# Another order for a recorded list of 6007 calls, and output stores that SyncE issues nearly alone

## The chip, the cores and the metric

The kernel runs on one core of a Trainium2 chip. A core has a matrix engine (TensorE, PE in the profile), three engines that work on 128 partitions of on-chip memory (VectorE or DVE, ScalarE or ACT, GpSimd or POOL), and a sync engine (SyncE or SP) that only issues DMA transfers and waits. Each runs its own list of instructions in order; they meet at semaphores. ScalarE and GpSimd can issue DMAs too. TensorE writes into PSUM (eight banks, used here as four rooms of two banks), and VectorE or ScalarE must copy the result to SBUF before the room can be used again; such a copy is called an evacuation below. The metric is the device time of one execution in microseconds (us), the median of several runs.

## The reference

Two long convolutions over L = 2048 positions for 448 channels are mixed by a gate, with x = `A_u` (2048 by 448, bfloat16):

```python
g = _sigmoid((x * gate_w).sum(-1, keepdims=True))
a = _A_ref(x, A_A_re, A_A_im, A_B_re, A_B_im, A_C_re, A_C_im, A_log_dt, A_Dskip)
b = _B_ref(x, B_k, B_v, B_shift_k, B_ssm_k, B_ssm_D)
return g * a + (1 - g) * b
# _A_ref: P = exp(dt*A*l); K = einsum("dn,dnl,dn->dl", C, P, dt*B).real   (256 modes, l < 2048)
#         y = irfft(rfft(u padded) * rfft(K padded))[:2048] + u * Dskip
# _B_ref: kv = (4-tap convolution of k with shift_k) * v
#         y = irfft(rfft(kv padded) * rfft(ssm_k padded))[:2048] + kv * ssm_D;  b = q * y, with q = x
```

So convolution A first has to make its own filter K from 256 complex modes per channel, and convolution B takes its filter as an input.

## The kernel before

**Transforms by matmuls.** A sequence of 2048 positions is held as 32 by 64, and the Fourier transforms are two stages of small matmuls with constant matrices: `spread` (matrix Wc), `transform` (W2), a product of two spectra on VectorE, then `stage_a` (R) and `stage_b` (G) back. `swapped` exchanges the two halves of the partitions by eight SyncE DMAs of 112 KB (`q<-q` in the profile). Nearly every matmul group ends with an evacuation PSUM to SBUF, and nearly all SBUF buffers lie in one tile of eight slots, named `q` in the profile.

**Quarters and plan.** The 448 channels are worked on in four quarters H = 0 to 3. A list, PLAN, gives the order in which the steps are recorded: T0, B0, B1, T1, B2, A0, T2, B3, p2, A1, T3, A2, m0, p3, A3. T is `table(H)`, which makes the filter of A: `exps` and `levels` on ScalarE (Exp, then Sin, with `minus` negating a part of the tile `ET`), `tables` as some 60 multiplies and adds on VectorE over the tiles TQ and TP, then matmuls (`sums`, `gather`, `spread_in`). B and A are the two convolutions of a quarter, p and m products with the gate. Before the plan stand the constants, the parameters (`Modes.run` transposes the six raw parameters and multiplies them into `hold`), and the short convolution of k, whose taps are loaded from `B_shift_k`, and whose transposed k lies where u (`natu`) is loaded afterwards.

**The gate.** 112 matmuls add up x * gate_w (calls 715 to 826, `ps<-natu,q`), one evacuation copies the sums to `gx` (call 827), one matmul adds partitions, and ScalarE takes a tanh into `gt` (call 829).

**The last stage.** `stage_b_shared` makes the quarters A1 to A3 together in six chunks of rows, b0 = 0, 12, 24, 36, 48 (12 rows each) and 60 (four rows). The function `together` evacuates each chunk to `natu` (128x1008, or 128x336 for the last four rows), multiplies it by the gate and adds it to `natv` on VectorE, and `store` writes it out in four DMAs, one for each 32 partitions (84 KB, or 28 KB).

**What sets the order.** Building the kernel first records all calls, numbered 0 to 6006, in a list. `Order.issue` then issues them in the sequence of the string ORDER, and chains each instruction to the one before it on its engine, so that the string alone decides each engine's order. This is why every row of the profile names line 153, the issuing line. Three more strings hold one character for each decision: SLOTS the slot of each SBUF buffer, ROOMS the PSUM room, and SIDES whether an evacuation (or a step of `levels`) goes to VectorE (V) or ScalarE (S). ScalarE must load a table before it can change between Exp or Tanh and Sin (`ACT_TABLE_LOAD`); copies need none. These loads are not in the string: they stand wherever the order changes from one kind to the other.

Of the kernel before, what the change touches and what calls it, by code (L numbers as in the profile page):

```python
# [40 lines left out]
    "3414351063757536613442666006711745305010456674026664531672"  # L41
)
ROOMS = (
    "23103002012223210321303300123103121213010301202302011203300011220312010002301113132311322332103320231330111003123323"
    "023300130213120112220103120310033231332213101032220302021200231110332111213100313200213312002"
)
SIDES = (
    "SSSSSSSSSSSSSSSSSSSSSSSSSSSSSSSSSSSSSSSSSSSSSVSSSSSSSSSSSSSSSSSSVVSVVVSSSSSSSSSSSSSSSSSSSSSSSSSSSSSSSSSSSSSSSSSSSSSS"
    "VVVVVVSSSSSSSSSSSSSSSSSSSSSSSSSSSSSSSSSSSSSSSSSVSSSSSSVVVVVVSSSSVSSVSSSSSSSSSSSSSSSSSSSSSSSSSSSVSSSSSSVSSSSSSS"
)  # L50
ORDER = (
# [688 lines left out]
def body(  # L740
# [20 lines left out]
    nc = Order(tc)  # L761
# [144 lines left out]
    ug = vt  # L906
# [33 lines left out]
    def store(b0, n):  # L940
        for g in range(4):
            dmae[g % 2].dma_start(out4[g][:, b0:b0 + n, :], ug[g * 32:(g + 1) * 32, b0:b0 + n, :])
# [132 lines left out]
```

## Time and profile before

| what | value |
|---|---|
| median of 3 runs (lowest to highest) | 245.65 us (245.57 to 247.34) |
| profiled execution | 246.74 us, its span 245.0 us |
| VectorE busy | 221.1 us, 370 instructions |
| ScalarE busy | 216.5 us, 301 instructions |
| TensorE busy | 199.1 us, 5134 matmuls |
| GpSimd busy | 23.7 us, 83 instructions |
| TensorE clock granted, mean | 0.962 |
| read from and written to device memory | 8.17 MB and 2.52 MB |

The span runs from the first to the last recorded instruction of the profiled execution; what lies around it is not in the trace. "Busy" adds up the time in which an engine was executing. Rows of the timeline give the start, the length, the engine, the operation with output and inputs and the shape, and in brackets how long the engine had been idle before, with what ended the wait. Rows of groups give the count, the busy time, the mean of one in ns, and the idle time before them.

### The profile page before, as it was taken

How to read it: one execution, taken by the hardware profiler on the slowest of the kernel's cores; microseconds unless marked ns; L12 is line 12 of the kernel's file. 1: busy time of each engine (PE TensorE's matmuls, PEld its weight loads, DVE VectorE, ACT ScalarE, POOL GpSimd, SP SyncE). 2: the span in 40 equal slices, each digit the busy share in tenths (PEclk: the TensorE clock that was granted, in tenths of full speed). 3: DMA queues.
4: the chain of work that ended last, by engine and by line, in shares of the span. 5: the costliest groups of instructions: out<-in, count | busy, mean ns of one | idle time of the engine just before them, and what ended most of it. 6: DMA issues, size and time to landing. Idle time of an engine off the chain costs nothing.

```text
span 245.0 us, 11464 instructions
## 1 busy us (share of the span) xinstructions
PE 199.1 (81%) x5134; PEld 177.4 (72%) x5134; DVE 221.1 (90%) x370; ACT 216.5 (88%) x301; POOL 23.7 (10%) x83
## 2 busy tenths in 40 slices
PE   0786888794989898986789989986999899889940
PEld 0732688784879798976688879985999888789730
DVE  7999998999679999999999999996999999878570
ACT  3899999899599999999999999989999979859550
POOL 8700001020000010200000111000012220000000
PEclk9997999799799999999999999997999999999995
DMA  6999999999430548445033756300073357130177
GB/s 141 200 188 198 159 134 162 168 169 234 131 99 5 136 82 145 80 95 138 5 49 62 168 108 137 90 5 4 5 152 80 78 96 172 42 80 3 21 155 126
DMA packets 59040, 26.37 MB, mean 108 GB/s; under 512 B 49648, under 2 KB 57328, under 8 KB 58992
## 3 DMA queue, kind: packets, MB, share of 16 engines
q1 hardware_dynamic: 52256, 18.65, 41.0%
q0 software_dynamic: 2160, 5.51, 12.8%
q10 hardware_dynamic: 4576, 1.49, 3.2%
q8 instruction: 40, 0.66, 1.2%
q14 instruction: 8, 0.07, 0.1%
HBM read 8.17 MB, written 2.52 MB: 44 GB/s over the span
## 4 chain that ended last, share of the span: by engine, by line
ACT 43%; DVE 22%; PE 16%; DMA 8%; issue 5%; SPq 3%; POOL 1%; ACTq 1%; DVEq 0%; POOLq 0%
ACT q L153 32%; PE ps L153 16%; DVE q L153 7%; DVE TP L153 6%; ACT ET L153 5%; DMA q<-q 4%; DMA q<-in_B_ssm_k_dram 4%; SPq L153 3%; ACT L153 2%; DVE natv L153 2%; DVE TQ L153 2%; DVE G L153 2%; DVE ET L153 2%; ACT natu L153 1%; ACT natv L153 1%
## 5 line engine op out<-in xcount | busy, mean ns | idle before, releaser
L153 ACT CAST q<-ps 128x1024 bf16<-128x1024 f32 (+4 forms) x182 | 149.2, 941 | 10.9 <-PE ps L153 9.7
L153 PEld LDWEIGHTS <-q 128*64 128x64 bf16 (+3 forms) x1168 | 65.4, 133 | 22.6 <-issue 10.0
L153 DVE TENSOR_TENSOR TQ<-TQ,ET 128x896 bf16<-128x896 bf16 (+2 forms) x70 | 45.8, 685 | 0.0
L153 PE MATMUL ps<-q,s_W 128*128 128x112 bf16 (+1 forms) x544 | 35.0, 214 | 6.7 <-ACT q L153 4.7
L153 DVE TENSOR_TENSOR q<-q 128x896 bf16<-128x896 bf16 (+2 forms) x32 | 37.6, 1202 | 1.4 <-ACT q L153 1.4
L153 PE MATMUL ps<-TP,TQ 128*32 128x32 bf16 x1792 | 33.2, 241 | 3.3 <-issue 1.7
L153 PEld LDWEIGHTS <-s_W 128*128 128x128 bf16 x544 | 28.5, 99 | 9.9 <-issue 7.3
L153 PE MATMUL ps<-sa_R,q 128*128 128x128 bf16 x448 | 32.4, 228 | 2.3 <-ACT q L153 0.7
L153 PEld LDWEIGHTS <-TQ 128*32 128x32 bf16 x1792 | 30.1, 153 | 5.6 <-issue 3.2
L153 DVE TENSOR_TENSOR TP<-TP,ET 128x1792 bf16<-128x1792 bf16 (+3 forms) x25 | 31.6, 1272 | 0.0
L153 PEld LDWEIGHTS <-natu 128*32 128x32 bf16 (+1 forms) x560 | 28.8, 183 | 3.7 <-issue 3.2
L153 POOL DMA_DIRECT2D TP<-TP x15 | 13.0, 867 | 151.8 <-PE ps L153 72.0
L153 ACT ACTIVATE q<-hold 128x224 bf16<-128x224 f32 x64 | 23.3, 438 | 0.7 <-DVE hold L153 0.7
L153 PEld LDWEIGHTS <-G 128*128 128x128 bf16 x512 | 16.4, 96 | 3.0 <-DVE q L153 0.7
L153 PE MATMUL ps<-q,G 128*128 128x56 bf16 (+2 forms) x512 | 17.4, 187 | 0.7 <-ACT q L153 0.7
L153 ACT ACTIVATE ET<-q 128x1344 bf16<-128x1344 int16 (+1 forms) x12 | 17.5, 1468 | 0.1
L153 DVE TENSOR_TENSOR TP<-TP,q 128x3584 bf16<-128x3584 bf16 (+1 forms) x10 | 16.4, 1645 | 0.0
L153 PE MATMUL ps<-Wc,natu 128*64 128x128 bf16 x224 | 15.8, 283 | 0.3 <-ACT q L153 0.2
L153 PE MATMUL ps<-Wc,natv 128*64 128x128 bf16 x224 | 15.0, 290 | 1.0 <-ACT q L153 1.0
L153 PEld LDWEIGHTS <-natv 128*64 128x64 bf16 x224 | 14.3, 213 | 1.6 <-DVE natv L153 0.5
L153 PE MATMUL ps<-q,natu 128*32 128x224 bf16 (+3 forms) x336 | 14.2, 283 | 1.5 <-ACT q L153 1.0
L153 DVE TENSOR_TENSOR TQ<-TQ 128x448 bf16<-128x448 bf16 (+2 forms) x35 | 15.2, 445 | 0.0
(75 smaller groups left out, 221.2 us busy)
## 6 DMA issues: line engine op xcount, KB each, us to landing
q<-q SPq DMA_DIRECT2D x64, 112.0 KB, 2.7
TP<-TP POOLq DMA_DIRECT2D x9, 448.0 KB, 5.5
natv<-in_B_v_dram SPq DMA_DIRECT2D x4, 448.0 KB, 7.4
q<-in_B_ssm_k_dram SPq DMA_DIRECT2D x16, 112.0 KB, 4.5
natu<-in_A_u_dram SPq DMA_DIRECT2D x4, 448.0 KB, 9.9
TP<-TP POOLq DMA_DIRECT2D x6, 224.0 KB, 3.5
out_dram<-natv SPq DMA_DIRECT2D x10, 84.0 KB, 2.8
out_dram<-natv ACTq DMA_DIRECT2D x10, 84.0 KB, 3.1
```

The lines of the kernel that those rows point to most:

```text
L153: ins = f(*args, **{k: x.ap() if isinstance(x, Both) else x for k, x in kw.items()})
```

## The change

SLOTS, ROOMS, SIDES and ORDER are replaced, and one line of `store` is changed. The list of recorded calls, their shapes and the plan are the same.

```diff
@@ store (and the strings SLOTS, ROOMS, SIDES, ORDER, not shown)
     def store(b0, n):
         for g in range(4):
-            dmae[g % 2].dma_start(out4[g][:, b0:b0 + n, :], ug[g * 32:(g + 1) * 32, b0:b0 + n, :])
+            (dmae[g % 2] if b0 in (0, 48) else nc.sync).dma_start(out4[g][:, b0:b0 + n, :], ug[g * 32:(g + 1) * 32, b0:b0 + n, :])
```

Of 24 stores SyncE issued 12 and ScalarE 12; now SyncE issues 20 and ScalarE four (two of chunk 0, two of chunk 48).

By SIDES, eleven operations move from ScalarE to VectorE: the copy of the gate sums (128x64), two negations of `ET` in T0 (128x896 and 128x672), two spreads of B0 and B1 (128x512), one 128x896 copy of A1's transform, four copies of the last 40 us (128x896, 128x1024 and two of 128x448), and the evacuation of the chunk b0 = 24. Three move the other way: a negation of `ET` in T1 (128x896), a 128x896 copy of A1 and a 128x448 copy of T3.

By ORDER, every engine's sequence changes throughout. Three places follow, with the issuing line printed as L153 before and L152 after.

The first is the start of the program on ScalarE. `TP<-TP 128x64` and `sa_R<-TP` are sines for constants, `TP<-TQ` an exponential of log_dt, `q<-hold` the exponentials of T0 and T1, `ET<-q` their sines, `s_W` and `TQ<-ps` sines for the matrices W2 and G, `q<-ps 128x896` evacuations. Before:

```order
2 L153 ACT_TABLE_LOAD
3 L153 ACTIVATE TP<-TP 128x64 x2
4 L153 ACT_TABLE_LOAD
5 L153 ACTIVATE TP<-TQ 128x448
6 L153 DMA q<-in_B_shift_k_dram 128x1792
7 L153 ACTIVATE q<-hold 128x224 x11
8 L153 COPY TQ<-ps_77 128x1792
9 L153 ACTIVATE q<-hold 128x224 x2
10 L153 ACTIVATE q<-q,quarter 128x3x224
11 L153 ACTIVATE q<-hold 128x224 x4
12 L153 ACT_TABLE_LOAD
```

The next table load of before stands at row 32, behind all of these sines. After, first the beginning and then the part with the loads between the sines:

```order
2 L152 ACT_TABLE_LOAD
3 L152 ACTIVATE TP<-TQ 128x448
4 L152 ACTIVATE q<-hold 128x224 x13
5 L152 COPY TQ<-ps_77 128x1792
6 L152 DMA q<-in_B_shift_k_dram 128x1792
7 L152 ACTIVATE q<-hold 128x224 x3
8 L152 ACTIVATE q<-q,quarter 128x4x224
9 L152 ACT_TABLE_LOAD
10 L152 ACTIVATE ET<-q 128x4x448
```

```order
19 L152 ACTIVATE ET<-q 128x3x448
20 L152 ACT_TABLE_LOAD
21 L152 ACTIVATE q<-hold 128x224 x2
22 L152 ACTIVATE q<-q,quarter 128x3x224
23 L152 ACT_TABLE_LOAD
24 L152 ACTIVATE ET<-q 128x3x448
25 L152 ACTIVATE TP<-TP 128x64
26 L152 ACT_TABLE_LOAD
27 L152 ACTIVATE q<-hold 128x224
28 L152 CAST q<-ps_79 128x896
29 L152 ACTIVATE q<-hold 128x224
30 L152 ACT_TABLE_LOAD
```

Up to the first evacuations the program has four table loads before and seven after (one more at row 36), and in all 9 before and 12 after. The load of the taps has moved behind the copy of the parameters (`TQ<-ps_77`): its buffer shares a slot with the raw A and B parameters now. On SyncE the loads of u stand, as before, behind the loads of B's filters.

The second place is the gate. Before, ScalarE copies the sums to `gx` (`q<-hold` exponentials, `q<-ps` evacuations; the tanh is `gt<-ps_77`):

```order
68 L153 ACTIVATE q<-hold 128x224 x3
69 L153 CAST q<-ps_76 128x128x4
70 L153 COPY gx<-ps_77 128x64
71 L153 CAST q<-ps_79 128x128x8
72 L153 ACTIVATE gt<-ps_77 128x64
73 L153 ACT_TABLE_LOAD
```

After, the copy is among VectorE's rows (TQ and TP rows are T0's tables, `q<-hold` the first level of T1):

```order
101 L152 TENSOR_TENSOR TP<-TP,q 128x3584
102 L152 TENSOR_TENSOR TQ<-TQ 128x448
103 L152 TENSOR_TENSOR TQ<-TQ,ET 128x2x2x224
104 L152 COPY gx<-ps_79 128x64
105 L152 TENSOR_TENSOR TQ<-TQ,ET 128x2x2x224
106 L152 CAST q<-ps_76 128x128x4
107 L152 TENSOR_SCALAR q<-hold 128x224 x3
```

VectorE copies the gate sums itself, near the end of T0's tables, and the evacuation of 128x512 that stood before the copy on ScalarE has come with it. On TensorE the gate sums stood in two pieces, 715 to 778 and 779 to 826, with the calls 1658 to 1665 and 1934 to 1941 (transforms of B0 and B1) between them and 1743 to 1758 (a spread of B1) behind. Now these 32 matmuls stand ahead, and all 112 gate sums stand in one piece behind them.

The third place is the end of the program on ScalarE and VectorE, the chunks of the last stage: `natu<-ps` is an evacuation, `natu<-natu,gates` the gate, `natv<-natv,natu` the add, `out_dram<-natv` a store. ScalarE before, from its last rows:

```order
262 L153 CAST natu<-ps_78 128x12x84
263 L153 DMA out_dram<-natv 32x12x112 x2
264 L153 CAST natu<-ps_77 128x12x84
265 L153 DMA out_dram<-natv 32x12x112 x2
266 L153 CAST natu<-ps_79 128x12x84
267 L153 DMA out_dram<-natv 32x12x112
268 L153 CAST natu<-ps_76 128x12x84
269 L153 DMA out_dram<-natv 32x12x112 x5
```

ScalarE after, and VectorE after:

```order
256 L152 CAST natu<-ps_79 128x12x84
257 L152 CAST natu<-ps_77 128x12x84
258 L152 CAST natu<-ps_76 128x12x84
259 L152 DMA out_dram<-natv 32x12x112
260 L152 CAST natu<-ps_78 128x12x84
261 L152 DMA out_dram<-natv 32x12x112 x3
```

```order
298 L152 TENSOR_TENSOR natu<-natu,gates 128x12x84
299 L152 TENSOR_TENSOR natv<-natv,natu 128x12x84
300 L152 CAST natu<-ps_79 128x12x84
301 L152 TENSOR_TENSOR natu<-natu,gates 128x12x84
302 L152 TENSOR_TENSOR natv<-natv,natu 128x12x84
```

The last evacuation, of the chunk b0 = 24, stands on VectorE, behind the add of the chunk before. TensorE makes the chunks in the order 60, 36, 24, 12, 48, 0 before and 60, 12, 48, 36, 0, 24 after. SyncE's last five stores, behind the last add, are three of chunk 24, one of chunk 0 and one of chunk 24.

More of the change, by code (lines that the diff above doesn't have):

```diff
@@ L40 @@
 SLOTS = (
-    "3414351063757536613442666006711745305010456674026664531672"
+    "0606540352707066242551222025744760322012651176021117531462"
 )
 ROOMS = (
-    "23103002012223210321303300123103121213010301202302011203300011220312010002301113132311322332103320231330111003123323"
-    "023300130213120112220103120310033231332213101032220302021200231110332111213100313200213312002"
+    "00211302012332132013332302331233311322002322001112002213010101231033123000201021202311021230110320120130010210312233"
+    "302012021032321213321331001130112211212322021112131031203213302021001000233333323322110233012"
 )
 SIDES = (
-    "SSSSSSSSSSSSSSSSSSSSSSSSSSSSSSSSSSSSSSSSSSSSSVSSSSSSSSSSSSSSSSSSVVSVVVSSSSSSSSSSSSSSSSSSSSSSSSSSSSSSSSSSSSSSSSSSSSSS"
-    "VVVVVVSSSSSSSSSSSSSSSSSSSSSSSSSSSSSSSSSSSSSSSSSVSSSSSSVVVVVVSSSSVSSVSSSSSSSSSSSSSSSSSSSSSSSSSSSVSSSSSSVSSSSSSS"
+    "SSSSSSSSSVSVSVSSSSSSSSSSSSSSSSSSSSSVSSSSSSSSSVSVSSSSSSSSSSSSSSSSVSSVVVSSSSSSSSSSSSSSSSSSSSSSSSSSSSSSSSSSSSSSSSSSSSSS"
+    "VVVVVVSSSSSSSSSSSSSSSSSSSSSSSSSSSSSSSSSSSSSSVSSSSSSSSSVVVVVVSSSSSSSVSSSSSSSSSVSSSVSSSSSSSSSSSVVVSSSSSSVSSSVSSS"
 )
 ORDER = (
[55 rows of a table removed]
[54 rows of a table added]
 )
```

109 rows, old and new, of the table ORDER are left out of this document.

## The prediction

> **What bounds the kernel now.** I read the page's busy shares first, then the chain that ended last, then stretches cut at events that the change touches, then the single waits.
>
> ```profile
> span 245.0 us, 11464 instructions
> PE 199.1 (81%) x5134; PEld 177.4 (72%) x5134; DVE 221.1 (90%) x370; ACT 216.5 (88%) x301; POOL 23.7 (10%) x83
> ACT 43%; DVE 22%; PE 16%; DMA 8%; issue 5%; SPq 3%; POOL 1%; ACTq 1%; DVEq 0%; POOLq 0%
> ```
>
> Three engines are over 80% busy, and the chain runs over ScalarE twice as long as over VectorE. No single engine is the bound; which of the two counts must be read stretch by stretch. The cuts below are the first multiply into `hold` (8.21), the end of the gate's tanh (68.8), T3's last sine (174.0), the end of T3's tables on VectorE (208.4) and the last add of the output (239.45).
>
> ```profile
> core 0: us, PE busy (x) PEld busy (x) DVE busy (x) ACT busy (x) POOL busy (x), PEclk, DMA share, GB/s
> 0.00:8.21 8.21, 0.93 (x8) 0.79 (x9) 5.93 (x38) 3.54 (x5) 6.85 (x56) 1.00 0.78 165
> 8.21:68.80 60.59, 49.35 (x934) 39.61 (x933) 56.93 (x86) 55.33 (x85) 6.03 (x14) 0.92 1.07 172
> 68.80:174.00 105.20, 92.12 (x2688) 84.98 (x2690) 100.68 (x145) 104.09 (x145) 5.12 (x6) 0.98 0.39 80
> 174.00:208.40 34.40, 32.03 (x866) 30.04 (x858) 34.25 (x74) 32.85 (x43) 5.74 (x8) 1.00 0.51 103
> 208.40:239.45 31.05, 24.71 (x660) 21.96 (x660) 23.29 (x31) 20.64 (x27) 0.00 (x0) 1.00 0.30 63
> ```
>
> Idle time is length less busy time. VectorE idles 2.28, 3.66, 4.52, 0.15 and 7.76 us in the five stretches, ScalarE 4.67, 5.26, 1.11, 1.55 and 10.41. So the third stretch belongs to ScalarE, the fourth to VectorE (T3's tables), the second to both by turns, and the last to a chain of TensorE, evacuation and stores. The profiled execution took 246.74 us, 1.74 outside its span; the median of the three runs shown is 245.65. I add my differences to the median.
>
> **The start, to the tanh at 68.8.** Three things change.
>
> ```profile
> 5.27 0.40 ACT L153 ACTIVATE TP<-TP 128x64 bf16<-128x64 int16 x2 [2.79 <-DVE TP L153]
> 5.69 1.28 ACT L153 ACT_TABLE_LOAD   x1
> 6.21 0.34 ACTq L153 DMA_DIRECT2D q<-in_B_shift_k_dram  x1
> 6.98 0.58 ACT L153 ACTIVATE TP<-TQ 128x448 bf16<-128x448 bf16 x1
> L153 ACT ACT_TABLE_LOAD x9 | 11.5, 1283 | 2.1 <-PEq L1059 1.2 <-DVE q L153 0.8
> 7.59 0.62 DVE L153 TENSOR_TENSOR hold<-ps,TP 128x448 f32<-128x448 bf16 x1 [0.47 <-ACT TP L153]
> PE ps L153 <- DMA q<-in_A_A_re_dram: 6.2, 1, 6.2
> ```
>
> First, the new order of ScalarE alternates Exp and Sin more often: 12 table loads instead of 9, all three new ones ahead of the first spreads. At 1.283 us each that is +3.85 us. Second, the multiply into `hold` cannot come earlier, since its transposes wait for the load of A_re (the 6.2 us row); VectorE did 5.93 us of constants up to its end, and those that stand ahead of it in the new order come to 3.2 by their rows. Its idle time there grows from 2.28 to about 4.65, and the moved work follows later: +2.4 us. Third, the taps (`B_shift_k`) share a slot with the raw parameters now and are issued behind the wide transposes, some 7 us later than 6.21; the short convolution slips, and the loads of `u`, which overwrite what it reads, with it.
>
> [...]
>
> Against this stands a stall that can go.
>
> ```profile
> natu<-in_A_u_dram SPq DMA_DIRECT2D x4, 448.0 KB, 9.9
> L153 SPq DMA_DIRECT2D natu<-in_A_u_dram x4: 2012/3122/3662, 42.3 to 51.3; - x4
> 61.42 0.78 PE L153 MATMUL ps<-natu,q 128*32 128x64 bf16 x20 [3.12 <-ACT q L153]
> 64.42 1.71 ACT L153 CAST q<-ps 128x896 bf16<-128x896 f32 x2 [2.84 <-PE ps L153]
> 67.46 0.46 DVE L153 TENSOR_SCALAR q<-hold 128x224 int32<-128x224 f32 x2 [2.00 <-PE ps L153]
> 67.55 0.22 ACT L153 COPY gx<-ps 128x64 f32<-128x64 f32 x1
> 68.56 0.26 ACT L153 ACTIVATE gt<-ps 128x64 f32<-128x64 f32 x1
> ```
>
> The last load of u is issued at 51.3 and takes about 9.9 us, so it lands at 61.2; TensorE, standing before the gate sums, had idled 3.12 us, ScalarE then 2.84 and VectorE 2.00 (the profile names a ScalarE copy that ends at 61.3; but the copy that frees the sums' room stands three copies earlier, and their first weight load waits for the four loads of u). In the new order 32 matmuls of a spread and two transforms (calls 1743 to 1758, 1658 to 1665, 1934 to 1941) come first, and all 112 gate sums stand in one piece behind them. That cover is about as long as u's new delay: the short convolution ended its matmuls at 42.1 and should end near 45.3, so u lands at 63.4 to 64.4, and the gate sums' 5 us (61.42 to the 66.4 of the last) end at 68.4 to 69.4. Their copy to `gx` is on VectorE now, with 63.5 us of work ahead of it by the rows; with 4.65 of idle, VectorE reaches it at 68.15. Both put the tanh at 68.5 to 69.5 against 68.56. What the start loses, the vanished stall pays: I take **0**. The ends are −2.84 (the stall goes, the start's slip hides in idle time) and +2.4 (the slip comes through).
>
> **From the tanh to T3's last sine.** Copies change sides; their prices:
>
> ```profile
> L153 ACT CAST q<-ps 128x896 bf16<-128x896 f32 x75 | 67.7, 957 | 5.5 <-PE ps L153 4.3 <-DVE natv L153 0.9
> L153 ACT CAST q<-ps 128x512 bf16<-128x512 f32 x22 | 14.2, 673 | 1.5 <-PE ps L153 1.4
> L153 ACT ACTIVATE ET<-ET 128x896 bf16<-128x896 bf16 x1 | 1.0, 963 | 0.0
> L153 ACT ACTIVATE ET<-ET 128x672 bf16<-128x672 bf16 x2 | 1.5, 770 | 0.4 <-DVE ET L153 0.4
> L153 DVE TENSOR_SCALAR ET<-ET 128x896 bf16<-128x896 bf16 x3 | 1.2, 387 | 0.0
> L153 DVE TENSOR_SCALAR ET<-ET 128x672 bf16<-128x672 bf16 x6 | 2.2, 369 | 0.1
> L153 DVE CAST q<-ps 128x896 bf16<-128x896 f32 x1 | 1.1, 1082 | 0.0
> L153 DVE CAST q<-ps 128x1024 bf16<-128x1024 f32 x2 | 2.4, 1218 | 0.3 <-PE ps L153 0.3
> L153 DVE CAST q<-ps 128x448 bf16<-128x448 f32 x2 | 1.2, 625 | 2.1 <-PE ps L153 2.1
> ```
>
> Ahead of the tanh, VectorE takes two negations of `ET` in T0 (0.39 and 0.37), two spreads of 128x512 (no row; between 0.63 for 448 and 1.08 for 896, nearer the first: 0.65 each) and the copy to `gx` (at most ScalarE's 0.22): +2.3, and ScalarE sheds 0.96, 0.77, twice 0.67 and 0.22, or 3.3, against the 3.85 of its table loads. Behind it, one negation of 128x896 in T1 comes back to ScalarE (+0.96; VectorE −0.39), and two 128x896 copies trade places. So in ScalarE's stretch ScalarE has **+1.0** us, with 1.1 of idle that could at best shrink; VectorE to the end of T3's tables has 2.3 − 0.4 = **+1.9**, with 4.5 idle us to take it. T3's own tables, 34.25 busy of 34.40, are the same calls before and after: 0. The end of T3 moves by 1.0 (ScalarE alone) to 1.9 (VectorE alone); I take **+1.3**, nearer ScalarE, whose copies into `q` lead the chain.
>
> **The tail.** Four copies move to VectorE between 208.4 and 228 (+3.3 us there); VectorE's 7.76 idle us hide them, and without that cover each costs the 0.13 us by which its copy is dearer. At the end:
>
> ```profile
> 235.64 1.00 ACT L153 CAST natu<-ps 128x1008 bf16<-128x1008 f32 x1 [0.78 <-DVE natu L153]
> 236.67 0.68 DVE L153 TENSOR_TENSOR natu<-natu,gates 128x1008 bf16<-128x1008 bf16 x1 [0.30 <-ACT natu L153]
> 236.81 1.00 ACT L153 CAST natu<-ps 128x1008 bf16<-128x1008 f32 x1 [0.18 <-issue]
> 238.77 0.68 DVE L153 TENSOR_TENSOR natv<-natv,natu 128x1008 bf16<-128x1008 bf16 x1
> 239.48 1.57 SPq L153 DMA_DIRECT2D out_dram<-natv  x3
> 239.49 0.93 ACTq L153 DMA_DIRECT2D out_dram<-natv  x2
> DMA  7779999998999999999999999995000000000010
> out_dram<-natv SPq DMA_DIRECT2D x6, 84.0 KB, 3.0
> ```
>
> The last two rows cover 236 to 246 in 40 slices. The last chunk (rows b0 = 24) is now evacuated by VectorE, behind the multiply and add of the chunk before. With TensorE's pace of about 1.75 us a chunk that add ends near 237.3 on the old clock; then 1.15 (between 1.08 and 1.22), 0.68, 0.10 and 0.68 lead to 239.9 instead of 239.45: +0.4. Then the stores. Behind the last add SyncE issued three and ScalarE two beside it; now five stand on SyncE, and ScalarE has nothing left. Three took 1.57 us, the last standing 0.90 behind the first, so 0.45 a step: four steps instead of two, +0.9. The transfers were still busy until 243 (slice 27), so part of the later issue falls into a queue that has emptied: −0.4, between −0.9 and 0. Tail **+0.9**, between 0 and +1.8.
>
> [...]
>
> **The sum**: 0 + 1.3 + 0 + 0.9 = +2.2, or 245.65 + 2.2 = **247.9 us**.
>
> **The rivals.**
> - *The gate stall pays more than the start costs.* ScalarE's 2.84 us idle goes, its new negation takes 0.96: T3 ends 1.9 early, the tail costs 0.9: 244.7. If the stores also hide in the transfers, 243.8 or a little less. For it: all three engines idle there at once. Against it: u is issued behind matmuls that slip. It decides if u lands by 62.
> - *The slip comes through.* VectorE has 2.4 more idle early and 1.9 more work, and no later idle time takes either: T3 ends 4.3 late, with the tail 5.2 late: 250.9. For it: VectorE idled only 8.3 us between 8 and 208, and 2.0 of them were the stall. Against it: ScalarE's copies, not VectorE, lead the chain there. It decides if the short convolution's matmuls end after 46.
> - *All this hides, only the tail shows*: 246.6. For it: ScalarE's 1.1 idle and VectorE's 4.5 are just large enough.
>
> **How the numbers follow.** A measurement of this kernel tells no less than 1% from no change: below 243.2 is faster, above 248.1 slower. Forecast 0.45, spread from 246.6 to 249.4 and lying so near the bound that I split it 0.25 within and 0.20 above. First rival 0.20 (0.10 below 243.2, if the stall's end and hidden stores come together, 0.10 within). Second 0.20, all above. Third 0.15, 0.13 within, 0.02 above. Faster 0.10, same 0.48, slower 0.42. For 8 in 10, the low end 244.0 leaves out half of the first rival, the high end 251.5 all but the worst of the second, where the taps hold VectorE a further while.
>
> **What would show it.** Right: 12 table loads, seven ahead of 45 us; VectorE idle some 4.6 us by its first `hold`; the gate sums without a wait of 3 us, the tanh between 68.5 and 69.5; T3's tables ending near 209.7; five stores on SyncE behind the last add, their last issue about 2 us after it. Wrong: a tanh before 67 or after 71, a T3 that ends earlier than 208, or a last landing no later after T3 than now (36.6 us, to the end of the span).

## The result, and the profile after

The changed kernel is slower: 256.07 us (253.15 to 259.4) against 245.88 (245.55 to 247.69) on the same chip, a ratio of 1.034 with a 95% interval of 1.026 to 1.042. The prediction, 247.9 with 244.0 to 251.5, is missed. (All ratios leave out executions that took over 1.5% more than the quickest of the same kernel, so the medians here lie further apart than the ratio.) Ratios are the measure below; 1% is 2.5 us.

The profiled execution of the changed kernel took 253.44 us, 1.84 outside its span, near the quick end of its executions; the others had a mean TensorE clock of 0.931 to 0.939 where it had 0.949 (before: 0.962). So its trace shows 6.6 us of the loss, and not all of it. From its page:

```profile
span 251.6 us, 11466 instructions
PE 200.9 (80%) x5134; PEld 178.6 (71%) x5134; DVE 226.8 (90%) x378; ACT 216.2 (86%) x296; POOL 23.7 (9%) x83
ACT 34%; DVE 28%; PE 24%; issue 7%; DMA 3%; SPq 1%; DVEq 0%; ACTq 0%
```

The busy sums hardly moved: ScalarE 0.3 us less, VectorE 5.7 more. What moved is the chain. TensorE had 16% of it and has 24%, about 60 us instead of 39; ScalarE fell from 43% to 34%. The same five stretches as in the prediction, cut at the same events:

```profile
core 0: us, PE busy (x) PEld busy (x) DVE busy (x) ACT busy (x) POOL busy (x), PEclk, DMA share, GB/s
0.00:7.46 7.46, 0.93 (x8) 0.80 (x9) 3.71 (x26) 1.86 (x2) 6.20 (x45) 1.00 0.74 162
7.46:70.34 62.88, 48.89 (x926) 39.22 (x927) 61.11 (x102) 58.22 (x87) 6.62 (x25) 0.92 0.97 156
70.34:179.17 108.83, 93.87 (x2670) 86.53 (x2668) 100.75 (x146) 105.79 (x145) 5.12 (x6) 0.95 0.40 84
179.17:213.45 34.28, 31.68 (x881) 29.49 (x878) 34.24 (x73) 31.28 (x41) 5.74 (x8) 1.00 0.51 103
213.45:245.51 32.06, 25.54 (x674) 22.60 (x670) 26.97 (x35) 19.03 (x25) 0.00 (x0) 1.00 0.28 60
```

The third stretch grew from 105.20 to 108.83 us. ScalarE's work there grew by 1.7 and its idle time from 1.11 to 3.04. VectorE has the same work as before, and its idle time grew from 4.52 to 8.08. TensorE's clock fell from 0.98 to 0.95. Smaller steps, from both traces (products are VectorE's multiplications of two spectra):

| end of (or start, where it says so) | before | after | later by |
|---|---|---|---|
| the short convolution's matmuls | 42.1 | 46.5 | 4.4 |
| the gate's tanh | 68.8 | 70.3 | 1.5 |
| B0's products | 79.0 | 82.1 | 3.1 |
| T1's tables | 115.3 | 118.4 | 3.2 |
| start of T2's table load on ScalarE | 117.1 | 121.4 | 4.4 |
| A0's products | 122.7 | 124.6 | 1.9 |
| start of B2's transform that waits (calls 2864 to 2871) | 120.9 | 125.3 | 4.4 |
| B2's products | 145.5 | 150.8 | 5.3 |
| T3's last sine | 174.1 | 179.2 | 5.1 |
| T3's tables | 208.4 | 213.5 | 5.0 |
| A2's products | 214.0 | 219.8 | 5.9 |
| last add | 239.45 | 245.51 | 6.1 |
| span | 245.0 | 251.6 | 6.6 |

**Ahead of T2.** The middle of the program loses first on ScalarE. From the tanh to the table load for T2's first sine it takes 51.10 us instead of 48.26 (before first, then after, the columns as above):

```profile
68.80:117.06 48.26, 42.74 (x1205) 39.21 (x1204) 47.36 (x68) 47.97 (x68) 2.56 (x3) 1.00 0.45 95
70.34:121.44 51.10, 43.86 (x1260) 40.46 (x1255) 49.02 (x70) 49.88 (x69) 2.56 (x3) 1.00 0.49 104
```

Of these 2.8 us, 1.9 are work that ScalarE now has ahead of the load: the negation that the prediction counted (0.94), and 19 copies of 128x896 instead of 18. The other 0.9 is idle time, most of it waiting for TensorE. This loss is steady. The 12 traces here that have the new middle take 50.5 to 53.5 us from the tanh to the load, and the eight with the old one 48.2 to 49.1. From the load to T3's last sine the changed kernel's trace loses only 0.7 more.

**T2's start.** Between A0's and B2's products the two traces differ by 3.4 us within 26. But A0's products are a poor mark, because VectorE now does them in one piece and they are only 1.9 late, while ScalarE's load and the waiting transform are 4.4 late. From that transform to B2's products 0.9 is lost. What changes there is the engine that leads. The chain of about 33 us around it, before first and then after, only the line of shares:

```profile
by line: ACT q L153 49.2%; ACT ET L153 11.7%; PE ps L153 11.3%; DVE TP L153 5.9%; DMA q<-q 5.7%; ACT natu L153 4.9%; issue 4.1%; ACT L153 3.9%; DVE natv L153 3.3%; DVE q L153 2.7%; DVEq L153 0.5%; ACTq L153 0.2%
```

```profile
by line: PE ps L152 24.3%; DVE TP L152 24.0%; DVE TQ L152 16.0%; DVE q L152 12.3%; ACT q L152 10.6%; issue 6.1%; ACT ET L152 5.1%; ACT L152 3.9%; DVEq L152 0.6%
```

Before, ScalarE's evacuations into `q` carried it; after, they have a tenth, and TensorE leads with VectorE behind it. TensorE's rows there, before:

```profile
118.28 1.68 PE L153 MATMUL ps<-TP,TQ 128*32 128x32 bf16 x96
120.92 0.56 PE L153 MATMUL ps<-q,s_W 128*128 128x112 bf16 x8 [0.96 <-ACT q L153]
```

and after, followed by three slices of 3 us of its windows (the columns as above):

```profile
121.61 0.71 PE L152 MATMUL ps<-TP,TQ 128*32 128x32 bf16 x32
122.25 0.57 PE L152 MATMUL ps<-q,s_W 128*128 128x112 bf16 x8
125.28 0.55 PE L152 MATMUL ps<-q,s_W 128*128 128x112 bf16 x8 [2.46 <-ACT q L152]
125.76 2.63 PE L152 MATMUL ps<-TP,TQ 128*32 128x32 bf16 x153
129.58 0.32 PE L152 MATMUL ps<-TP,TQ 128*32 128x32 bf16 x7 [1.19 <-issue]
129.83 0.93 PE L152 MATMUL ps<-q,s_W 128*128 128x112 bf16 x8
130.55 1.06 PE L152 MATMUL ps<-sa_R,q 128*128 128x128 bf16 x8
131.40 0.95 PE L152 MATMUL ps<-q,s_W 128*128 128x112 bf16 x8
...
123.00:126.00 3.00, 0.72 (x24) 0.63 (x27) 3.00 (x8) 3.00 (x4) 0.00 (x0) 1.00 0.00 0
126.00:129.00 3.00, 2.39 (x153) 2.28 (x146) 1.68 (x5) 3.00 (x5) 0.00 (x0) 0.63 0.03 5
129.00:132.00 3.00, 2.42 (x30) 2.37 (x30) 2.65 (x6) 2.71 (x4) 0.00 (x0) 0.50 0.74 118
```

B2's transform (calls 2864 to 2871) needs a PSUM room that ScalarE empties only after a table load of 1.28 us and T2's first sine of 1.70. Before, TensorE did 96 of T1's `sums` during that time and then waited 0.96 us. In the new order those sums stand behind the transform, and it waits 2.46. The longer wait is not itself the transform's delay, since ScalarE is 4.4 late by then; but more of TensorE's work stands behind it, and two more losses follow. The granted clock falls to one half for two periods of 3.4 us (0.63 and 0.50 in the slices), and the groups of eight matmuls take 0.93, 1.06 and 0.95 us where they take 0.57, 0.68 and 0.56 at full clock: 1.13 together. And TensorE stands 1.19 us for nothing that the profile names ("issue"). T1's last sums end at 134.48, and VectorE, whose next operation writes a tile that they read, waits for them:

```profile
134.52 0.28 DVE L152 COPY TP<-ET 128x448 bf16<-128x448 bf16 x1 [1.45 <-PE ps L152]
```

The clock records of both traces stand at 1.0 or 0.5, and each but the last of a trace is 3.41 us long or a multiple of that. How busy TensorE was ahead of half clock is in the last section.

**The start.** Rows of the changed kernel's ScalarE, SyncE and TensorE, with SyncE's loads of k into `natu` before as the first:

```profile
5.75 12.33 SPq L153 DMA_TRANSPOSE natu<-in_B_k_dram  x3
```

```profile
L152 ACT ACT_TABLE_LOAD x12 | 15.4, 1283 | 2.4 <-PEq L1058 1.2 <-DVE q L152 1.0
10.43 0.34 ACTq L152 DMA_DIRECT2D q<-in_B_shift_k_dram  x1
15.33 7.37 SPq L152 DMA_TRANSPOSE natu<-in_B_k_dram  x3
25.56 0.62 PE L152 MATMUL ps<-q,natu 128*32 128x448 bf16 x3 [4.61 <-DMA natu<-in_B_k_dram]
46.53 8.99 SPq L152 DMA_DIRECT2D natu<-in_A_u_dram  x4
65.36 3.56 PE L152 MATMUL ps<-natu,q 128*32 128x64 bf16 x112 [0.26 <-ACT q L152]
70.11 0.22 ACT L152 ACTIVATE gt<-ps 128x64 f32<-128x64 f32 x1 [2.00 <-PE ps L152]
```

The taps go out 4.2 us later. The transposed loads of k, which the prediction doesn't mention, also move: the three into `natu` start 9.6 us later, but all four loads of k together end only 2.0 later on SyncE (22.70 instead of 20.73). TensorE waits 4.61 us for them, and its first matmul on k starts at 25.56 instead of 24.87 (in `start_new` below at 24.75). So k explains little of the 4.4 us by which the short convolution ends late. Between, TensorE runs at half clock from 24.4 to 31.2 us and waits for ScalarE's evacuations (in `start_new` for 4.93 us in one piece, up to 34.85).

u comes hardly later: its last load is issued at 51.98 instead of 51.30 and lands at 61.53 instead of 61.22. The gate sums start without their wait of 3.12, as foreseen, but at 65.4 instead of 61.4, almost 4 us behind u. With the old start they begin 0.2 us behind its landing in seven traces; with the new one the work ahead of them holds them. ScalarE still idles 2.00 before the tanh. One trace tells little here: the tanh ends at 70.3 to 71.2 in the five traces with the new start, and at 67.3 to 71.4 in ten with the old one (68.6 on average).

### The profile page after: what moved, and what is told of

Same layout as the page of the kernel before. It is cut to its first block, busy times and chain, and to the rows that moved or that the text cites. A ratio compares the mean times of both kernels' runs of the same rounds, so it can differ in the third digit from the quotient of the medians.

```text
span 251.6 us, 11466 instructions
## 1 busy us (share of the span) xinstructions
PE 200.9 (80%) x5134; PEld 178.6 (71%) x5134; DVE 226.8 (90%) x378; ACT 216.2 (86%) x296; POOL 23.7 (9%) x83
## 4 chain that ended last, share of the span: by engine, by line
ACT 34%; DVE 28%; PE 24%; issue 7%; DMA 3%; SPq 1%; DVEq 0%; ACTq 0%
ACT q L152 27%; PE ps L152 24%; DVE q L152 8%; DVE TP L152 7%; DVE TQ L152 6%; ACT L152 3%; ACT ET L152 2%; DVE natv L152 2%; DMA q<-in_A_A_re_dram 2%; SPq L152 1%; DVE natu L152 1%; ACT natv L152 1%; DVE hold L152 1%; DMA q<-q 1%; DVE G L152 1%
## 5 line engine op out<-in xcount | busy, mean ns | idle before, releaser
L152 ACT CAST q<-ps 128x896 bf16<-128x896 f32 (+3 forms) x177 | 146.1, 960 | 12.6 <-PE ps L152 10.3
L152 PEld LDWEIGHTS <-q 128*64 128x64 bf16 (+3 forms) x1168 | 66.2, 133 | 14.8 <-DMA q<-in_A_A_re_dram 5.8
L152 DVE TENSOR_TENSOR TQ<-TQ,ET 128x896 bf16<-128x896 bf16 (+2 forms) x70 | 46.1, 690 | 0.0
L152 PE MATMUL ps<-q,s_W 128*128 128x112 bf16 (+1 forms) x544 | 35.0, 212 | 8.2 <-ACT q L152 7.4
L152 DVE TENSOR_TENSOR q<-q 128x896 bf16<-128x896 bf16 (+2 forms) x32 | 37.4, 1205 | 1.1 <-ACT q L152 1.0
L152 PE MATMUL ps<-TP,TQ 128*32 128x32 bf16 x1792 | 33.2, 241 | 5.8 <-issue 3.6
L152 PEld LDWEIGHTS <-s_W 128*128 128x128 bf16 x544 | 28.4, 99 | 12.0 <-issue 9.3
L152 PEld LDWEIGHTS <-natu 128*32 128x32 bf16 (+1 forms) x560 | 29.2, 183 | 10.8 <-DMA natu<-in_B_k_dram 5.1
L152 PEld LDWEIGHTS <-TQ 128*32 128x32 bf16 x1792 | 30.2, 154 | 7.9 <-issue 6.4
L152 PE MATMUL ps<-sa_R,q 128*128 128x128 bf16 x448 | 33.3, 233 | 0.4 <-DVE q L152 0.2
L152 DVE TENSOR_TENSOR TP<-TP,ET 128x1792 bf16<-128x1792 bf16 (+3 forms) x25 | 31.6, 1271 | 0.3 <-ACT ET L152 0.3
L152 POOL DMA_DIRECT2D TP<-TP x15 | 13.0, 867 | 154.6 <-PE ps L152 74.4
L152 ACT ACTIVATE q<-hold 128x224 bf16<-128x224 f32 x64 | 23.3, 448 | 2.6 <-DVE hold L152 2.6
L152 PE MATMUL ps<-q,natu 128*32 128x224 bf16 (+3 forms) x336 | 15.7, 300 | 7.2 <-DMA natu<-in_B_k_dram 4.6
L152 PEld LDWEIGHTS <-G 128*128 128x128 bf16 x512 | 16.6, 96 | 4.1 <-issue 2.0
L152 PE MATMUL ps<-q,G 128*128 128x56 bf16 (+2 forms) x512 | 17.7, 187 | 1.8 <-ACT q L152 1.2
L152 ACT ACTIVATE ET<-q 128x1344 bf16<-128x1344 int16 (+1 forms) x12 | 17.4, 1465 | 0.1
L152 PE MATMUL ps<-Wc,natv 128*64 128x128 bf16 x224 | 15.2, 295 | 1.8 <-DVE natv L152 1.1
L152 DVE TENSOR_TENSOR TP<-TP,q 128x3584 bf16<-128x3584 bf16 (+1 forms) x10 | 16.4, 1652 | 0.0
L152 PEld LDWEIGHTS <-natv 128*64 128x64 bf16 x224 | 14.6, 213 | 2.2 <-DVE natv L152 1.3
L152 PE MATMUL ps<-Wc,natu 128*64 128x128 bf16 x224 | 15.2, 283 | 0.9 <-ACT q L152 0.7
```

The lines of the kernel that those rows point to most:

```text
L152: ins = f(*args, **{k: x.ap() if isinstance(x, Both) else x for k, x in kw.items()})
```

## The experiments

Each ratio is against the kernel before on the same chip. Hybrids of the two orders take the slots, rooms and sides that go with each part. "Start" is all up to the tanh (call 829), "middle" from there to the end of T3's tables, "tail" the rest.

### Which part of the order carries the loss

`start_new`: the new start, then the old order and stores. `start_old`: the old start, then all of the new. `middle_new`: only the middle new. `tail_new`: only the tail and the stores new. `stores_only`: the old order with the new line in `store`.

```diff
 ORDER         to 829   to T3's tables   rest   store
-before        old      old              old    old
+start_new     new      old              old    old
+start_old     old      new              new    new
+middle_new    old      new              old    old
+tail_new      old      old              new    new
+stores_only   old      old              old    new
```

> The program up to the tanh of the gate in the order, sides and buffers of before, the rest as after (slots renamed so that lives do not collide; the same calls). Parts theory: the profile of after is 1.5 us late at the tanh and 3.1 us late at B0's products, so the start's share goes and about 256.1 - 3 = 253 us stays. Clock theory: the runs of after spread from 253 to 259 because stretches of half TensorE clock fall where TensorE is waited for, whatever the start; then the median stays at 255 to 257 and the spread stays several us wide.

> The reverse: up to the tanh as after (12 table loads, taps late, gate sums in one piece), the rest as before, stores alternating as before. Parts theory: 245.9 + 3 = 249 us. Forecast of the prediction (start costs nothing): 246. If the late start also lets the clock drop behind it, more than 250.

> Before up to the tanh, then the order of after up to the end of T3's tables, then before's rest and before's stores. Parts theory: after lost 2.0 us at the start of T2 (118 to 135 us) and nothing else between 76 and 213, so 245.9 + 2 = 248 us. Prediction's term for this stretch: +1.0 to +1.9, so 247 to 248. Rival: the loss in T2 follows from the late start and not from this order; then 246.

> Before up to the last of T3's table operations, then the order, sides and stores of after. Prediction's term: +0.9 (0 to +1.8), so 246.8 us. From the profile of after (T3's end to the end of the span 38.1 us, before 36.6): +1.5, so 247.4. Rival, stores hidden in the transfers: 246.

> The kernel before with nothing changed but the line of store: SyncE issues 20 of the 24 stores, in before's order. Prediction: the tail's issue term, +0.9 less up to 0.9 that the transfers hide, so +0.5 us (0 to +0.9). Rival: one queue of descriptors carries less than two, then +1 to +2 us. Third: no change within 0.3 us.

| kernel | median us | before | ratio, 95% |
|---|---|---|---|
| start_old | 253.3 | 247.13 | 1.025 (1.021 to 1.028) |
| start_new | 251.66 | 247.13 | 1.019 (1.017 to 1.022) |
| middle_new | 255.88 | 247.13 | 1.032 (1.024 to 1.040) |
| tail_new | 250.74 | 247.13 | 1.015 (1.010 to 1.021) |
| stores_only | 247.93 | 247.0 | 1.004 (1.001 to 1.008) |

By the losses in the profile, `start_old` was put at 253, `start_new` at 249, `middle_new` at 248 and `tail_new` at 247. Only the first came out so; the others are 2.7, 7.9 and over 3 us slower than that. Each part costs something by itself, and the parts sum to 6.6% where the whole costs 3.4. The middle is the largest and by itself nearly as slow as the whole. Some of that is the cut: in `middle_new` VectorE's first levels behind the tanh wait 4.0 us for ScalarE's `ET`, which the new start prepares earlier; in the whole changed kernel that wait is 1.0. The middle alone also shows both of the losses at T2's start, with a second stall of 1.31 us, and B2's products end 9.1 us late. VectorE's group behind the tanh in the changed kernel, then that group and two of TensorE's rows in `middle_new`:

```profile
L152 DVE TENSOR_SCALAR q<-hold 128x224 int32<-128x224 f32 x10 | 2.2, 273 | 1.2 <-ACT ET L152 1.0 <-PE ps L152 0.2
```

```profile
L156 DVE TENSOR_SCALAR q<-hold 128x224 int32<-128x224 f32 x8 | 1.8, 273 | 4.9 <-ACT ET L156 4.0 <-PE ps L156 0.8
125.09 0.91 PE L156 MATMUL ps<-q,s_W 128*128 128x112 bf16 x8 [2.42 <-ACT q L156]
134.03 0.71 PE L156 MATMUL ps<-TP,TQ 128*32 128x32 bf16 x32 [1.31 <-issue]
```

The profile of `tail_new` is 2.9 us late at the end of T3's tables already, behind calls in the old order: the gate sums, which wait for u, start at 64.0 there (between 60.2 and 64.0 in the traces with the same early code). So this lateness is within what executions with the same early code differ by. The part that is new takes 39.3 us, from T3's tables to the end of the span, where the kernel before takes 36.6.

### The table loads

`start_8loads` is `start_new` with four exponentials moved beside others, so that ScalarE loads 8 tables instead of 12:

```diff
-… 833 213 … 847 58 …        (836, 2145, 2138, 2140 further on)
+… 833 836 213 … 847 2145 2138 2140 58 …
```

> As start_new (median 251.7), but the Exps 836, 2145, 2138 and 2140 are moved beside other Exps, which takes four table loads out of the start (8 in all instead of 12). Load theory: 4 x 1.28 = 5.1 us of ScalarE, which stand ahead of evacuations of the short convolution; gate sums start near 62 again instead of 66.5, 247 to 248.5. Theory that the late taps and the late k set the start: no change, 251 to 252.

Measured 249.16 against 247.02, ratio 1.009 (1.005 to 1.012). The four loads, 5.1 us of ScalarE, were worth 2.5; they are half of what the new start costs. The result lies between the two forecasts, and the gate sums start at 65.0 and not near 62. The later loads of k and the taps stay, and so does the short convolution's end, at 45.9. What makes up the other half is not shown.

### T2's start: keep TensorE busy

`middle_fill` puts 40 matmuls with a result that nothing reads ahead of the waiting transform, `after_fill` does the same to the whole changed kernel:

```diff
 ORDER of the changed kernel
-… 2950-2958 3407 2864-2871 2854 …
+… 2950-2958 3407 6007-6046 2864-2871 2854 …
 recorded at the end, into a part of the PSUM room that is written over later
+for i in range(40): nc.tensor.matmul(room[:, 0, 448:512], lhsT=W2[:, i % 32] ..., rhs=Wc[:, 0:64], ...)
```

`middle_sums` and `after_sums` move 96 of T1's sums (2436-2467 and 2596-2659) to that place instead.

> As middle_new (median 255.9, before 247.1 on the same chip), but on TensorE 96 of T1's sums (calls 2436 to 2467 and 2596 to 2659) stand ahead of the transform matmuls 2864 to 2871, which wait 2.42 us for a ScalarE evacuation behind a table load and a sine. Wait theory: the wait shrinks by 1.7 us and so does the time: 254. Clock theory (that wait lets the granted clock fall to a half, and T1's sums and A0's stage_a then run at half speed to 139 us): A0's products to B2's products takes 23 to 25 us again instead of 30, and the time is 249 to 250.

> As middle_new, with 40 matmuls of 128x64 more on TensorE, which write PSUM columns that nothing reads, ahead of the same waiting matmuls 2864 to 2871. They do nothing for the result and leave every wait for ScalarE where it is; they only keep TensorE busy. Wait theory: nothing changes, 255 to 257. Clock theory: as good as moving the sums, 249 to 250.5.

> The kernel after with the same 96 sums moved ahead of 2864 to 2871. Clock theory: the T2 start of after (A0's products to B2's products 26.2 us, before 22.8) gets back 2 to 4 us, the median falls from 256 to 252 to 254, and the runs spread less than 253 to 259. Wait theory: at most 1.7 us, the spread stays.

> The kernel after with 40 useless matmuls ahead of the transform matmuls 2864 to 2871, as middle_fill. Clock theory: no half-clock window between 122 and 140 us, B2's products end 2 to 3 us after before's plus the start's 3 us (148 to 149 instead of 150.8 to 152.5), and the median falls from 1.041 of before (after: 256.1 to 245.9; after_hold 1.041) to 1.025. If not the clock but the order itself makes the loss: 1.035 to 1.045.

| kernel | median us | before | ratio, 95% | without the edit |
|---|---|---|---|---|
| middle_sums | 252.94 | 247.02 | 1.024 (1.016 to 1.031) | 1.032 |
| middle_fill | 252.52 | 247.02 | 1.020 (1.012 to 1.029) | 1.032 |
| after_sums | 254.28 | 247.02 | 1.020 (1.010 to 1.030) | 1.034 |
| after_fill | 251.27 | 246.9 | 1.018 (1.009 to 1.027) | 1.034 |

All four are quicker, by 0.8 to 1.6%, two of them by adding work that is thrown away. No pair is apart by its intervals alone (those of `after` and `after_fill` just touch, the others overlap), and the two middles end between the forecasts of the two theories, so the size, up to half of the loss, is rough. What supports the verdict is that all four went the same way, and the clock in the traces:

| new middle | half-clock periods between 120 and 140 us | us from T2's load to T3's last sine |
|---|---|---|
| with 40 useless matmuls: `after_fill`, `middle_fill`, `after_fill_8loads` | none | 56.5, 56.5, 58.6 |
| with 96 sums or 66 useless matmuls: `middle_sums`, `after_sums`, `after_mended` | one each | 58.8, 60.4, 61.8 |
| without: the changed kernel, `after_hold`, `middle_new`, `middle_hold`, `after_hold_8loads`, `start_old` | two each | 57.7, 61.2, 61.5, 61.8, 62.2, 62.4 |

The eight traces with the old middle have none there; seven take 57.0 to 58.4 us, and `before_fill` 61.0. The groups also differ in B2's late transfer (below), so the times are not the clock's alone. The loss of the new middle behind T2's load, unlike the one ahead of it, differs much from trace to trace, and the changed kernel's profiled execution has one of the smallest. `after_fill`, TensorE's rows, its slices of 3 us and its chain at the same place:

```profile
122.45 1.33 PE L155 MATMUL ps<-Wc,s_W 128*128 128x64 bf16 x40
125.10 0.55 PE L155 MATMUL ps<-q,s_W 128*128 128x112 bf16 x8 [1.32 <-ACT q L155]
125.58 2.69 PE L155 MATMUL ps<-TP,TQ 128*32 128x32 bf16 x160
128.20 0.57 PE L155 MATMUL ps<-q,s_W 128*128 128x112 bf16 x8
...
126.00:129.00 3.00, 3.00 (x163) 2.90 (x156) 1.87 (x5) 3.00 (x4) 0.00 (x0) 1.00 0.02 5
129.00:132.00 3.00, 2.30 (x113) 2.26 (x113) 2.65 (x6) 2.98 (x5) 0.00 (x0) 1.00 0.80 122
...
by line: ACT q L155 66.9%; ACT ET L155 11.9%; ACT L155 8.3%; issue 6.9%; PE ps L155 4.1%; ACT natu L155 2.9%; ACTq L155 0.6%
```

The transform comes no earlier (125.10, since the room is freed by ScalarE as before), but the clock stays at 1.00, the groups take 0.57 again, the stall of 1.19 is gone, and the chain runs over ScalarE. B2's products end 1.7 us earlier (149.05 instead of 150.78). Elsewhere half clock comes up as before: 24.5 us in the whole trace, where the changed kernel has 25.9. One thing is not separated: 40 more matmuls also shift which instruction the "issue" stalls fall on, so clock (1.13) and stall (1.19) vanished together.

`after_fill_8loads` adds the regrouped tables to that; `after_mended` has them with 40 useless matmuls ahead of the gate sums and 66 ahead of the transform; `before_fill` puts 194 into the old order, at five places where TensorE waits.

```diff
 before_fill, useless matmuls ahead of     1510   715   2855   4560   4551
+                                            36    88     24     30     16
 after_mended, ahead of                     715  2864
+                                            40    66
```

> The kernel after with the two causes found so far treated at once: four table loads taken out of the start (8 in all), and useless matmuls (40 ahead of the gate sums, 66 ahead of the waiting transform 2864 to 2871 at T2's start) that keep TensorE busy through its waits. If loads (2.5 us by start_8loads against start_new) and clock (3 us by middle_fill against middle_new) are the causes, 256.1 - 5.5 = 250 to 251 us and a spread of 2 us; if they overlap, 252 to 253; if not, 255 or more.

> The kernel before with 194 useless matmuls in its longer TensorE waits (36 ahead of the first spread of B0, 88 ahead of the gate sums, 24 at T2's start, 46 at T3's start). Clock theory: the half-clock stretches behind these waits (45 to 51, 60 to 66 and 168 to 174 us) go or shrink, 1 to 3 us less than before, 243 to 245. Rival: TensorE is not waited for there, or the waits fall elsewhere: within 0.5 us of before.

> The same with four table loads taken out of the start (8 instead of 12). Start and T2 as separate causes: another 1 to 2.5 us less than after_fill, 1.015 to 1.02 of before. If the windows fall as chance has it, no better than after_fill.

All three missed. `after_mended`: 254.3 against 247.0, 1.021 (1.016 to 1.026). `after_fill_8loads`: 253.31 against 246.9, 1.025 (1.017 to 1.033). `before_fill`: 253.34 against 247.0, 1.025 (1.019 to 1.031), which is 6 us lost. A row or two of `before_fill` and then of `after_fill_8loads`:

```profile
44.76 1.44 PE L157 MATMUL ps<-Wc,s_W 128*128 128x64 bf16 x24 [3.06 <-ACT q L157]
150.45 1.79 PE L157 MATMUL ps<-sa_R,q 128*128 128x128 bf16 x12 [3.45 <-DVE q L157]
```

```profile
145.92 3.96 DVE L155 TENSOR_TENSOR q<-q 128x3584 bf16<-128x3584 bf16 x2 [2.47 <-ACT q L155]
210.74 1.65 PE L155 MATMUL ps<-q,s_W 128*128 128x112 bf16 x16 [2.24 <-issue]
```

In `before_fill` a useless matmul itself waited 3.06 us for an evacuation of its room, with the work behind it. A wait of 3.45 appeared at 147, where the last of B2's transfers between partition halves had taken 5.45 us (next section). In `after_fill_8loads` A0's products are back at the old time (122.6), but VectorE then waits 2.47 us at B2's products, and an "issue" stall of 2.24 at 208.5 is followed by half clock at 210. So far as these traces show it, what one place gains another wait takes.

### B2's halves and T2's transfer

In `middle_new` and `start_old` the last of B2's eight transfers between partition halves (112 KB) lands 5.6 and 6.0 us after its issue, where it takes 2.3 to 2.4 before and after; in those two GpSimd's first transfer for T2 (448 KB) was issued 0.8 and 1.0 us ahead of it. The other traces agree: 5.1 to 6.0 us in the five in which GpSimd's transfer went first and the landing is known, 2.3 to 4.5 in the 13 in which it came second. The hold lets GpSimd copy four columns of the swapped data first:

```diff
-… 2884 2987 …      (3436, GpSimd's first transfer, further ahead)
+… 2884 6007 3436 2987 …      6007: nc.gpsimd.tensor_copy(mark, four columns of B2's slot)
```

> As middle_new, but GpSimd reads four elements of B2's swapped half (a copy of 128x4 into a tile that nothing uses) before it issues the first accumulate DMA of T2 (448 KB), so that this DMA cannot start until the eight swap DMAs of B2 have landed. Collision theory (last swap DMA of B2 lands 2.3 us after its issue if issued before that accumulate, 5.1 to 6.0 us if behind it; middle_new: issued 0.8 us behind, 5.6 us): B2's products start near 147.5 instead of 150.6, and the median falls from 255.9 by about 3 us to 253. Clock theory alone: nothing changes, or later by the accumulate's delay.

> The kernel after with the same hold. In after's profile the last swap DMA of B2 was issued 0.5 us ahead of the accumulate and landed in 2.3 us, in a run of 253.4; its other runs go to 259.4. Collision theory: runs above 255.5 are those that lost this race; with the hold the slow half goes, the median falls from 256 to 253 to 254 and the spread to 2 or 3 us. Otherwise median 256, spread as before.

> The kernel before with the hold (both first accumulate DMAs of T2 wait for B2's swap). Before wins the race in its profile by 0.4 us (last swap DMA at 137.7, accumulate at 138.1). Collision theory: its runs of 249 to 251 us go, the median of 247.0 falls by 0 to 0.5, unless T2's tables then wait for the later accumulate (up to +2).

> After with the hold and with four table loads taken out of its start (8 instead of 12). Loads (2.5 us by start_8loads against start_new) and collision (about 2 to 3 us) together: 250.5 to 252. If the loads only shift the race, 253 to 256.

Against 247.85: `middle_hold` 256.6, 1.036 (1.031 to 1.042); `after_hold` 257.63, 1.041 (1.036 to 1.046); `before_hold` 247.89, 1.005 (1.000 to 1.010); `after_hold_8loads` 256.74, 1.036 (1.030 to 1.041). Nothing is gained. In `middle_hold` the transfers take 2.3 us again and B2's products end 3.4 us earlier than in `middle_new` (151.1 against 154.5), but GpSimd starts T2's transfer only at 148.98 instead of 143.70, and T2's tables end at 168.3 instead of 168.5. The late transfer is real, and this hold moved the wait to VectorE's tables. The hold is no remedy. That the late transfer costs nothing is not shown by it, because the hold also puts T2's transfer off by 5.3 us; a shorter one was not tried.

### The stores

`tail_oldstores` is `tail_new` with the old line in `store`:

```diff
-(dmae[g % 2] if b0 in (0, 48) else nc.sync).dma_start(...)
+dmae[g % 2].dma_start(...)
```

> As tail_new (before up to T3's tables, then after's order and sides), but with the stores alternating between SyncE and ScalarE as before. If the stores make the tail's loss (tail_new: 39.3 us from T3's end to the end of the span, before 36.6), it goes back to about 37; if the order and VectorE's evacuation of the last chunk make it, it stays at 38 to 39.

Measured 252.32 against 247.0, 1.021 (1.016 to 1.025), where `tail_new` has 1.015 (1.010 to 1.021): the intervals overlap. The profiles point the same way: from T3's tables to the last add 34.9 us with the old stores and 32.8 with the new. ScalarE in `tail_oldstores`:

```profile
232.83 3.27 ACTq L155 DMA_DIRECT2D out_dram<-natv  x4
236.14 1.90 ACT L155 CAST natu<-ps 128x1008 bf16<-128x1008 f32 x2 [2.47 <-PE ps L155]
239.09 1.00 ACT L155 CAST natu<-ps 128x1008 bf16<-128x1008 f32 x1 [1.05 <-DVE natv L155]
```

The second row is put down to TensorE, but ScalarE was in its stores until 236.10: a store waits in line for VectorE's add, and the next evacuation waits behind it. So in the new tail the new stores seem to help, and in the old tail they cost 0.4%.

## Why the prediction was wrong, point by point

- **"From the tanh to T3's last sine", +1.0 to +1.9, is the step that failed.** The trace has +3.6 in that stretch. The prediction gave ScalarE 1.0 us of work there, "with 1.1 of idle that could at best shrink". Its work grew by 1.7, and its idle time did not shrink but grew, from 1.11 to 3.04: a new order can make an engine wait longer for another, and for that the sum had no term. Of the 3.6, 2.8 stand ahead of T2's table load (1.9 of work, 0.9 of idle time). Behind it the trace has 0.7 more, and other traces with the new middle up to 5; half clock, stalls and B2's late transfers stand there, and what each costs is not separated. The clock column of the stretches was quoted (0.92 and 0.98) and not read: it says that TensorE not only waited but also ran at half clock (in the trace of before for 3.41 us each from 45.25, 62.32 and 168.13, each time behind 3.41 us in which its matmuls were busy for 0.90 to 1.81 us).
- **"whose copies into `q` lead the chain"** held before, and ceased around T2's start: their share of the chain there fell from 49 to 11%. A new order can change which engine leads, so that prices by the old leader no longer apply.
- **The start, 0**, is mis-sized. The trace has +1.5 at the tanh, and `start_new` 1.9% by itself. The three table loads were counted, but the vanished gate stall did not pay for them. "u lands at 63.4 to 64.4" failed: it landed at 61.53, and still the gate sums came 4 us late, because the work ahead of them did. The multiply into `hold`, which "cannot come earlier", ended at 7.46 instead of 8.21 (its row names an idle time of 0.47 us ended by ScalarE). So VectorE's early idle time came to 3.75 where 4.65 was expected. The taps came 4.2 us later and not 7. 12 table loads, seven of them ahead of 45 us, are as predicted, and four loads were worth 2.5 us, half of their time.
- **T3's tables, 0**: right, 34.28 us long against 34.40.
- **The tail, +0.9**: the trace has +1.6 from T3's tables to the end of the span, within the 0 to 1.8 given. Of this, 0.8 stands already at A2's products, where TensorE has another stall (the row, and SyncE's last stores):

```profile
212.64 0.57 PE L152 MATMUL ps<-q,ga_sel 128*32 128x56 bf16 x33 [1.81 <-issue]
242.63 5.56 SPq L152 DMA_DIRECT2D out_dram<-natv  x10
```

  So the size came out partly by luck. Five stores stood behind the last add (245.51), as predicted, and the last was issued by 248.19. From the last add to the end of the span it is +0.6, where the prediction had +0.5 (0.9 of issue less 0.4). The line's own cost, 0.4% in the old order, agrees with this too, but its sign seems to turn in the new tail. The four copies that move to VectorE come to 3.55 us by the rows shown, not 3.3; the sum doesn't use them.
- **The rivals.** "The slip comes through" was nearest with 250.9, and its condition was met (the short convolution ended at 46.5), but not what it described: it had VectorE's idle time used up, and that grew from 4.52 to 8.08 us between the tanh and T3's last sine. So its nearness is luck. That the order could make ScalarE and TensorE wait longer for each other was no rival at all.

**What stays open:** what the start costs beside its table loads; how the loss behind T2's load splits between clock, stall and late transfer; why the parts don't add; and some 2 to 3 us by which the medians of the changed kernel lie above its profiled execution, where only the lower clocks (0.931 to 0.939) are known. Over the 20 traces the time at half clock (from 28 us after the start of the span to 14 us before its end) goes from 7 to 31 us and follows the span with a correlation of 0.87, but this doesn't say which of the two makes the other.

## What to carry to other kernels

When an order is changed, look at every place where TensorE waits for an evacuation and ask what else it had to do there: in the changed kernel a wait of 2.46 us at T2's start was followed by two periods of 3.41 us at half clock, in which three groups of matmuls took 1.13 us longer together. The idle time of the engine that leads is not only room to shrink: a new order can make it grow. Price a changed order by the engine that leads after the change, not by the one that led before. A gain at one wait (table loads, an earlier transfer, filler) counts only once the next thing behind it is shown to be ready.

## What the runs showed of the hardware

**Half clock followed periods in which TensorE was partly idle.** The clock records of the 20 traces were cut into their periods of 3.41 us, and those taken that begin at least 28 us after the start of the span and end at least 14 us before its end. A period at full clock was followed by half clock as follows (busy with matmuls or weight loads):

| TensorE busy in the period | periods | followed by half clock |
|---|---|---|
| under 50% | 46 | 45 |
| 50 to 60% | 41 | 26 |
| 60 to 70% | 63 | 19 |
| 70 to 75% | 36 | 2 |
| over 75% | 918 | 0 |

So of the 63 periods with 1.0 to 1.4 us of idle time (60 to 70% busy), 19 were followed by half clock. Where the periods begin differs from one trace to the next, also among kernels with the same start: at the gate, half clock begins at 62.3 in `before`, at 61.8 in `tail_new` and at 59.9 in `stores_only` (the last two worked out from slices of 3 us), and lasts two periods in `tail_new` and one in the others. Not all matmuls took longer: 128 of the 32-column sums take 2.16 us at full clock (119.01 in the changed kernel) and 2.19 in a stretch mostly at half (132.29), while the groups of 112 and 128 columns there take over 1.5 times as long (0.93 against 0.57, 1.06 against 0.68).

**The longer "issue" waits of TensorE stood at one place in the count of its records.** The waits view of before and of after (total, times, longest):

```profile
PE ps L153 <- issue: 4.2, 7, 1.2
```

```profile
PE ps L152 <- issue: 6.9, 8, 1.8
```

```profile
q8 instruction: 40, 0.66, 1.1%
```

Counted along all of TensorE's records (matmuls, weight loads, and some 60 semaphore and drain records), with the count begun anew after every 256, all 95 such stalls over 0.5 us in the 20 traces stand at number 193 or 194. In the changed kernel's trace there are six, of 0.52 to 1.81 us. Its page (last row: packets, MB) counts 40 transfers of the kind "instruction". Each of the 95 stalls ends 1.2 to 1.9 us after the end of one of these (the six 1.24 to 1.50). No run changed these transfers alone, so whether they make the stalls is not shown. A changed order, or 40 useless matmuls, moves the work on which the stalls fall: the one of 1.19 at 129.58 in the changed kernel is gone in `after_fill`.
